# Pooled attention with two gated stages on one Trainium2 core: the attention probabilities turned by one block transpose and six DMAs through DRAM in place of twenty transposes a head pair

## Chip, cores and metric

One core of one Trainium2 chip. The metric is the device time of one execution in microseconds (us). A difference under about 0.3% (4.5 us here) is taken as no change.

## What is computed

Attention over pooled keys and values, then two dense stages; all in float32.

```
k_p = k.reshape(B, H, Sp, 8, D).mean(axis=3);  v_p likewise        # B, H, S, D = 8, 8, 576, 64; Sp = 72
attn = softmax(q @ k_p^T / sqrt(D));  out = attn @ v_p              # x: (B*S, H*D) = (4608, 512)
x = ((x @ w1) * (x @ w2) @ w3) @ w_out                              # 512 -> 1024 -> 1024 -> 512
h = x @ w_in;  y = (h * sigmoid(1.702 h)) @ w_out2                  # 512 -> 2048 -> 512
```

## The kernel before

**Stages.** Every float32 product is made of three matmuls (`mm3`, L112 to L116): each operand is split into a high part (a rounding cast by ScalarE) and a low part (the difference, by VectorE or GpSimd, L103 to L105). In a first stage weights are loaded, rounded apart (`Conv`, L127) and `w3 @ w_out` is formed (L508, L114 to L116 into `acc`). In a second, nine blocks of 512 tokens go through the gated product: for each of eight column tiles `f` 12 + 12 matmuls into `wk[0]` and `wk[1]` (L624), a copy of `wk[0]` by ScalarE (L638), the product with `wk[1]` by VectorE (L641), a split, and two tiles later 12 matmuls into `acc` (`x2_step`, L585). A third stage (L709) does the last two matrices by a Strassen-like scheme.

**The attention groups.** There are 32 groups, one for two heads of one batch entry, numbered 0 to 31. They run between the pieces of the first two stages, by `tick` (L432): a tick is called twice a column tile, and four ticks belong to a group, so that a group takes two tiles. In a group: `g0` transposes k and q in 32x32 blocks (L255, L256) and sums keys; `g1` makes ten score matmuls of 144 columns (L278), takes the maximum (L283) and subtracts it (L285); `g2` is the exponential (L294); `g3` normalizes (L300 to L303, in `s_t`, 128 tokens x 5 tiles x 160 columns) and turns the probabilities to the keys' partitions; `g4` splits the turned tiles `p0` (128 keys) and `p1` (the other 16 of 144, in 32 rows) into `ph` and `pt` (L368 to L372); `g6` multiplies by the pooled values (L380 to L383, 288 columns each) and writes x (L390, L391). `g_va` and `g_vb` (L318, L336) pool the values on GpSimd, out of one buffer `vr` that `v_load` refills.

**The turn.** Groups 0 to 3 are turned by TensorE (L351 to L361). From group 4 on, L310 to L316 issue 20 VectorE transposes a group, each of 32 partitions, 28 groups x 20 = 560.

**The order of the work.** The program is written in the order above, but a scheduler puts each engine's instructions in order by its own estimate of times. Each engine's queue then runs in order; all loads and stores of this part are issued in order by SyncE (SP), and a DMA that must wait holds those behind it. An order given below is read from the built program.

Of the kernel before, what the change touches and what calls it, by code (L numbers as in the profile page):

```python
# [7 lines left out]
F32 = mybir.dt.float32  # L8
# [4 lines left out]
ALU = mybir.AluOpType  # L13
# [4 lines left out]
P = 128  # L18
# [4 lines left out]
def pooled_attention_moe_moe2(  # L23
# [26 lines left out]
    HP = H // 2  # L50
# [18 lines left out]
    dr_p = ctx.enter_context(tc.tile_pool(name="dr", bufs=1, space=DRAM))  # L69
# [30 lines left out]
    def f32(ap):  # L100
        return ap.bitcast(F32)
# [22 lines left out]
    def sl(i, n=P):  # L124
        return slice(i * n, (i + 1) * n)
# [65 lines left out]
    with pa_ctx:  # L191
        pa = pa_ctx.enter_context(tc.tile_pool(name="pa", bufs=1))
        cv_p[0] = pa


        mask = pa.tile([P, 2, D], F32, name="mask")
        nc.gpsimd.memset(mask, 1.0 / POOL)
        nc.gpsimd.affine_select(
            out=mask[:, 0], in_=mask[:, 0], compare_op=ALU.is_gt, fill=0.0,
            base=SK, pattern=[[0, D]], channel_multiplier=-1)  # L200
        nc.gpsimd.affine_select(
            out=mask[:, 1], in_=mask[:, 1], compare_op=ALU.is_ge, fill=0.0,
            base=-SK, pattern=[[0, D]], channel_multiplier=1)
        qT = pa.tile([P, TT * P], F32, name="qT")
        nc.vector.memset(qT[:, S:], 0.0)
        kbd = pa.tile([P, 2, SK], F32, name="kbd")
# [4 lines left out]
        for t in s_ts:  # L211
# [6 lines left out]
            out=ident, in_=ident, compare_op=ALU.is_equal, fill=0.0,  # L218
            base=0, pattern=[[-1, P]], channel_multiplier=1)
# [14 lines left out]
        def g_load(n):  # L234
            if n >= NG:
                return
            b, hp = divmod(n, HP)
            g_k[n] = pa.tile([P, S], F32, name="kr", tag="raw", bufs=4).rearrange("p (g d) -> p g d", d=32)
            load_blocks(g_k[n], k, b, hp)
            g_q[n] = pa.tile([P, S], F32, name="qr", tag="raw", bufs=4).rearrange("p (g d) -> p g d", d=32)  # L240
            load_blocks(g_q[n], q, b, hp)

        def v_load(n):
            if n >= NG:
                return
            b, hp = divmod(n, HP)
            vr = v[b, 2 * hp:2 * hp + 2].rearrange("h (s u) d -> (h s) (u d)", u=POOL)
            g_v[n] = pa.tile([P, POOL * D], F32, name="vr", tag="vr")
            nc.sync.dma_start(g_v[n], vr[:P])
            nc.sync.dma_start(vtr[:KT], vr[P:])  # L250

        def g0(n):
            kr, qr = g_k.pop(n), g_q.pop(n)
            kT = pa.tile([P, S], F32, name="kT", tag="kT")
            nc.vector.transpose(out=kT, in_=kr.rearrange("p g d -> p (g d)"))  # L255
            nc.vector.transpose(out=qT[:, :S], in_=qr.rearrange("p g d -> p (g d)"))  # L256
            ks = pa.tile([P, SK], F32, name="ks", tag="ks")
# [38 lines left out]
        def g3(n):  # L296
            r, s_t = g_s.pop(n), s_of(n)
            pv = s_t[:, :, :KW].rearrange("p t (a s) -> p t a s", s=SK)
            rv = r.rearrange("p (t a) -> p t a", a=2)
            nc.vector.tensor_reduce(out=rv, in_=pv, op=ALU.add, axis=AX.X)  # L300
            nc.vector.tensor_scalar_add(r, r, 1e-9)
            nc.vector.reciprocal(out=r, in_=r)
            nc.vector.tensor_tensor(  # L303
                out=pv, in0=pv, in1=rv.unsqueeze(3).to_broadcast([P, TT, 2, SK]), op=ALU.mult)
            p0 = pa.tile([P, TT, P], F32, name="p0", tag="p0")
            p1 = pa.tile([32, TT, P], F32, name="p1", tag="p1")
            g_s[n] = (p0, p1)
            if n < NPE:
                return
            for r in range(5):  # L310
                for c in range(4):
                    nt = TT if 32 * (c + 1) <= S - (TT - 1) * P else TT - 1
                    dst = p0[32 * r:32 * r + 32] if r < 4 else p1[:32]
                    nc.vector.transpose(  # L314
                        out=dst[:, :nt, 32 * c:32 * c + 32],
                        in_=s_t[32 * c:32 * c + 32, :nt, 32 * r:32 * r + 32])  # L316

        def g_va(n):  # L318

            vr, tr = g_v.pop(n), vtr  # L320
            a = pa.tile([P, 4 * D], F32, name="va", tag="va")
            at = pa.tile([32, 4 * D], F32, name="vat", tag="vat")
            for d, s in ((a, vr), (at, tr)):
                nc.gpsimd.tensor_tensor(out=d, in0=s[:, :4 * D], in1=s[:, 4 * D:], op=ALU.add)
                nc.gpsimd.tensor_tensor(
                    out=d[:, :2 * D], in0=d[:, :2 * D], in1=d[:, 2 * D:], op=ALU.add)
                nc.gpsimd.tensor_tensor(out=d[:, :D], in0=d[:, :D], in1=d[:, D:2 * D], op=ALU.add)
            vf = pa.tile([P, 2, D], F32, name="vf", tag="vf")
            nc.gpsimd.tensor_tensor(
                out=vf, in0=a[:, :D].unsqueeze(1).to_broadcast([P, 2, D]), in1=mask, op=ALU.mult)  # L330
            vtf = pa.tile([32, D], F32, name="vtf", tag="vtf")
            nc.gpsimd.tensor_scalar_mul(vtf, at[:, :D], 1.0 / POOL)
            g_v[n] = (vf.rearrange("p a d -> p (a d)"), vtf)
            v_load(n + 1)

# [9 lines left out]
        def g4(n):  # L345
            p0, p1 = g_s.pop(n)
            if n < NPE:
                ps, s_t = banks_of(n), s_of(n)
                p0f, p1f = (t.rearrange("p t c -> p (t c)") for t in (p0, p1))
                for tt in range(4):  # L350
                    nc.tensor.transpose(ps[0][:, sl(tt)], s_t[:, tt, :P], ident)  # L351
                nc.scalar.copy(p0f[:, :T], ps[0])
                w = S - T
                nc.tensor.transpose(ps[1][:, :w], s_t[:w, 4, :P], ident[:w, :w])
                for tt in range(3):
                    nc.tensor.transpose(
                        ps[1][:32, w + tt * P:w + (tt + 1) * P], s_t[:, tt, P:], ident)
# [8 lines left out]
            s0 = p0.rearrange("p t c -> p (t c)")[:, :S]  # L366
            s1 = p1.rearrange("p t c -> p (t c)")[:, :S]
            nc.scalar.copy(ph[:, 0], s0)  # L368
            nc.gpsimd.tensor_tensor(out=ph[:, 1], in0=s0, in1=f32(ph[:, 0]), op=ALU.subtract)
            nc.scalar.copy(pt[:32], s1)  # L370
            nc.scalar.copy(pt[32:64], s1)
            nc.gpsimd.tensor_tensor(out=pt[64:96], in0=s1, in1=f32(pt[:32]), op=ALU.subtract)  # L372

        def g6(n):
            b, hp = divmod(n, HP)
# [226 lines left out]
        for blk in range(NB):  # L602
            x = [x_slot(blk, c) for c in range(KM)]
            if blk == NB - 2:

                pa_ctx.close()
                pa = pa_ctx.enter_context(tc.tile_pool(name="pc", bufs=1, reuse_waits="tile"))
# [10 lines left out]
            for f in range(NF1):  # L618
# [18 lines left out]
                a = pa.tile([P, T], F32, name="a", tag="a", bufs=2)  # L637
# [34 lines left out]
    with tc.tile_pool(name="pb", bufs=1, reuse_waits="tile") as pb, \  # L672
# [196 lines left out]
        x = x_first  # L869
# [9 lines left out]
        for k, f in enumerate(FO):  # L879
            bk = bank()  # L880
            w = ready.pop(("h", 0, f))
# [8 lines left out]
            g = moving()[:, :, 0]  # L890
# [20 lines left out]
        for pr in range(1, NPAIR + 1):  # L911
# [17 lines left out]
            for fp in range(NFP):  # L929
# [4 lines left out]
                for name, i in ORDER:  # L934
# [6 lines left out]
                    if name in PART:  # L941
                        s, h = PART[name]
                        w = ready[s, pr, 2 * fp + i][:, h]
                    else:
                        w = ready[name, pr, fp][:, i]
# [10 lines left out]
                    elif name == "M2":  # L956
# [42 lines left out]
            src = {"M5": 0, "M7": 1, "M3": 2, "M2": 3, "M4": 3, "M6": 4}  # L999
# [129 lines left out]
```

## Time and profile before

| | us |
|---|---|
| median of 3 runs (1480.33 to 1484.5) | 1483.54 |
| the profiled execution | 1480.04 |
| its span, first to last instruction | 1478.3 |
| TensorE busy in the span | 1437.1 (97%) |
| VectorE busy | 991.5 (67%) |
| ScalarE busy | 696.6 (47%) |
| GpSimd busy | 491.9 (33%) |

PE is TensorE's matmuls, PEld its weight loads, DVE VectorE, ACT ScalarE, POOL GpSimd, SPq SyncE's queue, which issues DMAs. A busy share is an average over stages that have different limits, so it has to be read stage by stage; and an engine that is always busy is at its limit only if its instructions also come at their full pace. Times in the trace count from the span's start.

### The profile page before, as it was taken

To read this page: it belongs to the slowest core of one execution; us is meant where nothing else is said; L and a number is where in the kernel's file an instruction comes from. 1 tells how busy PE (TensorE), PEld (TensorE's weight loads), DVE (VectorE), ACT (ScalarE), POOL (GpSimd) and SP (SyncE) were. 2 spreads that over 40 slices of the span, in tenths; PEclk is the share of its full clock that TensorE was granted. 3 is DMA by queue.
4 is the path that set the end of the run, shared out by engine and by line. 5 is a ranking of instruction groups with operands and counts; after the bars stand their busy time and mean duration, and the time that the engine had idled before them with its cause. 6 is when DMAs were issued, how large, how long until landed. Compare 5 with 4: busy or idle time off the path is not lost.

```text
span 1478.3 us, 19409 instructions
## 1 busy us (share of the span) xinstructions
PE 1437.1 (97%) x6536; PEld 1188.0 (80%) x6536; DVE 991.5 (67%) x1728; ACT 696.6 (47%) x1212; POOL 491.9 (33%) x589
## 2 busy tenths in 40 slices
PE   5978999999999999999999999999999999999998
PEld 3766888888888888888888887888788888888886
DVE  7889998878787877645636345783559354954554
ACT  6974444434343434366635334652455244634442
POOL 8787865555555555357743200000000000000000
PEclk9989999999999999999999999999999999999999
DMA  9992333323232321089869978877677766785665
GB/s 275 243 227 41 65 81 61 77 49 77 47 75 48 74 41 37 29 295 337 329 230 391 330 240 306 292 213 225 200 237 223 224 199 216 241 237 179 196 213 141
DMA packets 294434, 267.63 MB, mean 181 GB/s; under 512 B 201664, under 2 KB 226240, under 8 KB 294336
## 3 DMA queue, kind: packets, MB, share of 16 engines
q1 hardware_dynamic: 291648, 265.09, 60.0%
q10 hardware_dynamic: 2688, 1.31, 0.3%
q8 instruction: 52, 0.85, 0.2%
q14 instruction: 46, 0.38, 0.1%
HBM read 209.72 MB, written 56.62 MB: 180 GB/s over the span
## 4 chain that ended last, share of the span: by engine, by line
PE 82%; DVE 7%; DMA 5%; ACT 2%; POOL 2%; issue 1%; SPq 1%; DVEq 0%; ACTq 0%; POOLq 0%
PE bk L709 39%; PE wk L114 8%; PE wk L116 8%; PE wk L115 8%; PE acc L114 4%; PE acc L115 4%; PE acc L116 4%; PE wk L278 2%; DMA wud<-wt 2%; DVE s L105 1%; DVE cv L169 1%; PE bk L114 1%; PE bk L115 1%; PE bk L116 1%; POOL cv L172 1%
## 5 line engine op out<-in xcount | busy, mean ns | idle before, releaser
L709 PE MATMUL bk<-xM,st 128*128 128x512 f32 x1140 | 269.1, 390 | 1.8 <-DMA st<-wind 1.3
L709 PE MATMUL bk<-mv,st 128*128 128x512 f32 x1104 | 258.7, 389 | 0.5 <-DMA st<-wud 0.5
L709 PEld LDWEIGHTS bk<-xM,st 128*128 128x128 f32 x1140 | 213.6, 188 | 48.0 <-issue 1.9
L709 PEld LDWEIGHTS bk<-mv,st 128*128 128x128 f32 x1104 | 207.1, 188 | 44.2 <-ACT mv L104 0.9
L114 PE MATMUL wk<-s,s 128*128 128x512 f32 x576 | 227.3, 396 | 6.1 <-DVE a L641 4.1
L116 PE MATMUL wk<-s,s 128*128 128x512 f32 x576 | 225.2, 391 | 0.9 <-DVE s L105 0.9
L115 PE MATMUL wk<-s,s 128*128 128x512 f32 x576 | 225.3, 392 | 0.1
L314 DVE STREAM_TRANSPOSE p<-s_t 32x160 f32<-32x160 f32 (+1 forms) x560 | 178.3, 318 | 10.5
L115 PE MATMUL acc<-s,s 128*128 128x512 f32 x352 | 141.2, 401 | 1.0 <-POOL s L105 0.8
L116 PE MATMUL acc<-s,s 128*128 128x512 f32 x352 | 140.7, 400 | 1.6 <-DVE s L105 1.6
L114 PE MATMUL acc<-s,s 128*128 128x512 f32 x352 | 134.1, 406 | 8.1 <-DVE s L105 5.4
L114 PEld LDWEIGHTS wk<-s,s 128*128 128x128 f32 x576 | 108.5, 189 | 30.1 <-DVE a L641 5.4
L116 PEld LDWEIGHTS wk<-s,s 128*128 128x128 f32 x576 | 108.5, 188 | 23.8 <-DVE s L105 1.1
L115 PEld LDWEIGHTS wk<-s,s 128*128 128x128 f32 x576 | 108.5, 188 | 22.1 <-DVE s L391 0.5
L105 POOL TENSOR_TENSOR s<-a,s 128x512 fp32r<-128x512 f32 x56 | 73.3, 1309 | 155.2 <-ACT s L104 121.4
L105 DVE TENSOR_TENSOR mv<-g,mv 128x1024 fp32r<-128x1024 f32 x80 | 97.8, 1222 | 32.5 <-ACT mv L104 31.0
L104 ACT CAST mv<-g 128x1024 fp32r<-128x1024 f32 x80 | 84.5, 1056 | 71.3 <-PE bk L709 70.8
L172 POOL TENSOR_TENSOR cv<-cv,s 128x512 int32<-128x512 int32 x72 | 100.8, 1408 | 33.6 <-DVE cv L169 24.2
L114 PEld LDWEIGHTS acc<-s,s 128*128 128x128 f32 x352 | 67.9, 194 | 23.3 <-ACT s L104 4.7
L116 PEld LDWEIGHTS acc<-s,s 128*128 128x128 f32 x352 | 67.9, 193 | 15.8 <-DVE s L105 2.7
L115 PEld LDWEIGHTS acc<-s,s 128*128 128x128 f32 x352 | 68.0, 193 | 14.4 <-POOL s L105 2.0
L638 ACT COPY a<-wk 128x512 f32<-128x512 f32 x72 | 42.1, 585 | 68.3 <-PE wk L116 68.1
(188 smaller groups left out, 2344.6 us busy)
## 6 DMA issues: line engine op xcount, KB each, us to landing
st<-wud SPq DMA_DIRECT2D x92, 512.0 KB, 4.3
st<-wind SPq DMA_DIRECT2D x66, 512.0 KB, 4.6
st<-wind SPq DMA_DIRECT2D x84, 256.0 KB, 3.8
s<-in_moe_w_dram SPq DMA_DIRECT2D x32, 512.0 KB, 6.5
wind<-s SPq DMA_DIRECT2D x32, 512.0 KB, 5.5
s<-in_moe_w_out_dram SPq DMA_DIRECT2D x24, 512.0 KB, 6.9
s<-wud SPq DMA_DIRECT2D x20, 512.0 KB, 4.3
kr<-in_k_dram SPq DMA_DIRECT2D x128, 72.0 KB, 2.5
```

Of the source, the lines that this page charges most:

```text
L104: nc.scalar.copy(dst[:, 0], src)
L105: lo_eng.tensor_tensor(out=dst[:, 1], in0=src, in1=f32(dst[:, 0]), op=ALU.subtract)
L114: nc.tensor.matmul(o, a[:, 0, a_sl], b[:, 0, b_sl], start=first, stop=False)
L115: nc.tensor.matmul(o, a[:, 0, a_sl], b[:, 1, b_sl], start=False, stop=False)
L116: nc.tensor.matmul(o, a[:, 1, a_sl], b[:, 0, b_sl], start=False, stop=last)
L169: nc.vector.tensor_scalar(out=wu, in0=e.bitcast(U32), scalar1=3, scalar2=None, op0=ALU.logical_shift_left)
L172: nc.gpsimd.tensor_tensor(out=w.bitcast(I32), in0=w.bitcast(I32), in1=lo_w.bitcast(I32), op=ALU.add)
L278: nc.tensor.matmul(sc[half][:, i * KW:(i + 1) * KW], qT[:, sl(tt)], mov, start=True, stop=True)
L314: nc.vector.transpose(out=dst[:, :nt, 32 * c:32 * c + 32], in_=s_t[32 * c:32 * c + 32, :nt, 32 * r:32 * r + 32])
L638: nc.scalar.copy(a, pa_)
L709: nc.tensor.matmul(o, w[:, x, m], b[:, y], start=first and n == 0, stop=last and n == 2, skip_group_check=True)
```

## The change

Groups 8 to 31 (`n >= NPT`, `NPT = 2 * HP = 8`) turn their probabilities in another way; 24 of the 28 groups that were turned by VectorE. One transpose of 128 partitions (128 x 800 elements, `pT`) turns each 32x32 block in its place. Four DMAs, of 32 partitions each, write it to a DRAM tile `pD` (two buffers) in the keys' order, and two DMAs read it back as `p0` (320 KB) and `p1` (80 KB). So that tokens come out in order, q's transpose goes in two pieces into columns ordered by half and block (`turn_q`), and `g4` reads 2 x 288 of 640 columns. In these groups the two subtractions of `g4` go from GpSimd to VectorE. For all groups, `g_va` sums in place in `vr` and `vtr` (so `vr` is read until the masked product, not until the first sum), and the mask has one column, broadcast.

```diff
+        def turn_q(n, qr):
+            if n < NPT:
+                nc.vector.transpose(out=qT[:, :S], in_=qr.rearrange("p g d -> p (g d)"))
+                return
+            dst = qT.rearrange("p (t h e j) -> p e h t j", h=2, e=2, j=32)
+            src = qr.rearrange("p (h g) d -> p h g d", h=2)
+            for e, g0_, g1_ in ((0, 0, TT), (1, TT, SB // 2)):
+                nc.vector.transpose(out=dst[:, e, :, :g1_ - g0_], in_=src[:, :, g0_:g1_])
...
-            for r in range(5):
-                for c in range(4):
+            if n < NPT:
+                for r in range(5):
+                    for c in range(4):
...
+                return
+            turned = pa.tile([P, 5, TT, 32], F32, name="pT", tag="pT")
+            nc.vector.transpose(
+                out=turned.rearrange("p r t j -> p t r j"),
+                in_=s_t.rearrange("p t (r k) -> p t r k", k=32))
+            d = dr_p.tile([5, 32, 4, PC], F32, name="pD", tag="pD", bufs=2)
+            for c in range(4):
+                nc.sync.dma_start(
+                    d[:, :, c].rearrange("r k x -> k r x"),
+                    turned[32 * c:32 * c + 32].rearrange("p r t j -> p r (t j)"))
+            nc.sync.dma_start(
+                p0.rearrange("p t c -> p (t c)"), d[:4].rearrange("r k c x -> (r k) (c x)"))
+            nc.sync.dma_start(
+                p1.rearrange("p t c -> p (t c)"), d[4].rearrange("k c x -> k (c x)"))
...
-            for d, s in ((a, vr), (at, tr)):
-                nc.gpsimd.tensor_tensor(out=d, in0=s[:, :4 * D], in1=s[:, 4 * D:], op=ALU.add)
...
+            for d in (vr, tr):
+                for w in (4 * D, 2 * D, D):
+                    nc.gpsimd.tensor_tensor(
+                        out=d[:, :w], in0=d[:, :w], in1=d[:, w:2 * w], op=ALU.add)
...
-            nc.gpsimd.tensor_tensor(out=ph[:, 1], in0=s0, in1=f32(ph[:, 0]), op=ALU.subtract)
...
+            late = n >= NPT
+            lo = nc.vector if late else nc.gpsimd
...
+            nc.scalar.copy(by_half(ph[:, 0]), s0)
+            lo.tensor_tensor(out=by_half(ph[:, 1]), in0=s0, in1=by_half(f32(ph[:, 0])), op=ALU.subtract)
```

The change moves instructions on every queue. Line numbers in the orders after the change are those of the changed kernel: L332 the block transpose, L337 the writes to `pD`, L340 and L342 the reads, L399 to L402 the casts of `g4`, L400 and L403 its subtractions, L315 the normalization, L423 the x writes, L670 and L673 the copy of `wk[0]` and the product with `wk[1]` (L638 and L641 before).

**Place 1, group 19, from its normalization on.** VectorE before (12 of the 20 transposes' rows shown, with the x writes of the group ahead, L391, between them):

```order
L303 TENSOR_TENSOR s_t<-s_t,nm 128x5x144
L314 STREAM_TRANSPOSE p_3971<-s_t 32x5x32 x2
L391 TENSOR_TENSOR s_3187<-wk_72,s_3187 128x256
L314 STREAM_TRANSPOSE p_3971<-s_t 32x4x32 x2
L314 STREAM_TRANSPOSE p_3971<-s_t 32x5x32 x2
L314 STREAM_TRANSPOSE p_3971<-s_t 32x4x32 x2
L391 TENSOR_TENSOR s_3913<-wk_73,s_3913 128x288
L314 STREAM_TRANSPOSE p_3971<-s_t 32x5x32 x2
L314 STREAM_TRANSPOSE p_3971<-s_t 32x4x32 x2
```

VectorE with the change:

```order
L315 TENSOR_TENSOR s_t<-s_t,nm 128x5x144
L332 STREAM_TRANSPOSE pT<-s_t 128x5x5x32
L423 TENSOR_TENSOR s_3088<-wk_72,s_3088 128x256
L423 TENSOR_TENSOR s_3766<-wk_73,s_3766 128x288
L423 TENSOR_TENSOR s_3766<-wk_72,s_3766 128x32
L400 TENSOR_TENSOR ph<-p_3823,ph 128x576
L673 TENSOR_TENSOR a<-wk_71,a 128x512
L403 TENSOR_TENSOR pt<-p_3824,pt 32x576
L295 TENSOR_REDUCE nm<-wk_72 128x6
```

SyncE's queue in the same stretch with the change (before, it held the loads of v, k and q alone):

```order
L337 DMA pD<-pT 32x5x160 x4
L249 DMA vr<-in_v_dram 128x512
L250 DMA vtr<-in_v_dram 16x512
L340 DMA p_3823<-pD 128x640
L342 DMA p_3824<-pD 32x640
L229 DMA kr<-in_k_dram 32x18x32 x4
L229 DMA qr<-in_q_dram 32x18x32 x4
```

The transposes are gone; the subtraction L400, which waits for data that has gone through DRAM, now stands ahead of the product L673 in VectorE's queue.

**Place 2, ScalarE in group 16,** from the casts of `g4` on. Before:

```order
L368 CAST ph<-p_3419 128x576
L370 CAST pt<-p_3420 32x576
L371 CAST pt<-p_3420 32x576
L638 COPY a<-wk_70 128x512
L104 CAST s_3472<-a 128x512
```

With the change:

```order
L399 CAST ph<-p_3307 128x576
L401 CAST pt<-p_3308 32x576
L670 COPY a<-wk_70 128x512
L402 CAST pt<-p_3308 32x576
L104 CAST s_3349<-a 128x512
```

The copy of `wk[0]` stands behind casts that wait for `p0` and `p1` in both; with the change so in groups 8, 12 and 16 (behind both) and 20 and 24 (behind the first), in the other late groups ahead of them.

**Place 3, SyncE in the first stage,** from the loads of k and q for the third group on. Before:

```order
L229 DMA qr<-in_q_dram 32x18x32 x4
L249 DMA vr<-in_v_dram 128x512
L250 DMA vtr<-in_v_dram 16x512
L151 DMA s_412<-in_moe_w_dram 128x1024
L151 DMA s_447<-in_moe_w_dram 128x1024
```

With the change:

```order
L151 DMA s_648<-in_moe_w_dram 128x1024
L151 DMA s_679<-in_moe_w_dram 128x1024
L151 DMA s_755<-in_moe_w_dram 128x4x256
L249 DMA vr<-in_v_dram 128x512
L151 DMA s_786<-in_moe_w_dram 128x4x256
L250 DMA vtr<-in_v_dram 16x512
```

The second load of v comes seven weight loads later than before.

## Rows read from the trace of the kernel before

**Rows 1.** Windows: us, then busy us of each engine, PEclk, DMA share, GB/s

```profile
80.00:120.00 40.00, 32.66 (x137) 26.02 (x138) 35.85 (x51) 28.88 (x64) 35.07 (x42) 0.87 1.01 197
120.00:160.00 40.00, 35.85 (x166) 29.29 (x166) 35.62 (x73) 17.61 (x37) 33.79 (x37) 1.00 0.18 34
160.00:200.00 40.00, 39.45 (x190) 32.53 (x189) 37.25 (x94) 16.72 (x39) 26.95 (x44) 1.00 0.39 90
240.00:400.00 160.00, 160.00 (x773) 135.37 (x772) 127.38 (x315) 63.10 (x142) 86.40 (x126) 1.00 0.29 61
400.00:600.00 200.00, 200.00 (x964) 169.20 (x964) 161.54 (x395) 78.45 (x178) 101.04 (x147) 1.00 0.24 54
600.00:880.00 280.00, 279.94 (x1246) 231.77 (x1245) 140.74 (x215) 139.45 (x242) 121.46 (x94) 1.00 0.80 280
```

**Rows 2.** Timeline of DVE: normalization of group 8; last transposes of group 31

```profile
193.38 0.90 DVE L303 TENSOR_TENSOR s_t<-s_t,nm 128x720 f32<-128x720 f32 x1
...
617.65 0.96 DVE L314 STREAM_TRANSPOSE p<-s_t 32x160 f32<-32x160 f32 x3
```

**Rows 3.** Timeline of PE, group 20 and the start of 21: start, us

```profile
399.09 1.39 PE L278 MATMUL wk<-kbd,qT 128*128 128x144 f32 x10
...
417.77 1.39 PE L278 MATMUL wk<-kbd,qT 128*128 128x144 f32 x10
418.89 0.49 PE L114 MATMUL wk<-s,s 128*128 128x512 f32 x1
...
421.76 0.39 PE L114 MATMUL wk<-s,s 128*128 128x512 f32 x1
...
425.16 0.29 PE L380 MATMUL wk<-ph,vm 128*128 128x288 f32 x1
```

**Rows 4.** Groups by line and form: xcount | busy us, mean ns

```profile
L314 DVE STREAM_TRANSPOSE p<-s_t 32x160 f32<-32x160 f32 x280 | 93.5, 334 | 6.2
L314 DVE STREAM_TRANSPOSE p<-s_t 32x128 f32<-32x128 f32 x280 | 84.8, 303 | 4.3
...
L256 DVE STREAM_TRANSPOSE qT<-qr 128x576 f32<-128x576 f32 x32 | 24.6, 768 | 0.0
...
L105 DVE TENSOR_TENSOR xM<-sx,xM 128x512 fp32r<-128x512 f32 x32 | 23.0, 720 | 2.9 <-ACT xM L104 2.8
...
L105 DVE TENSOR_TENSOR s<-cv,s 128x512 fp32r<-128x512 f32 x12 | 16.0, 1336 | 1.2 <-ACT s L104 1.2
```

**Rows 5.** Timeline of DVE, same group, from its normalization

```profile
406.68 0.90 DVE L303 TENSOR_TENSOR s_t<-s_t,nm 128x720 f32<-128x720 f32 x1
...
417.65 0.69 DVE L641 TENSOR_TENSOR a<-wk,a 128x512 f32<-128x512 f32 x1 [2.13 <-ACT a L638]
```

**Rows 6.** Timeline of ACT, same group, casts and copy

```profile
416.33 0.67 ACT L371 CAST pt<-p 32x576 fp32r<-32x576 f32 x1
417.03 0.59 ACT L638 COPY a<-wk 128x512 f32<-128x512 f32 x1
```

**Rows 7.** Timeline of POOL, same group, the second subtraction

```profile
416.53 1.42 POOL L372 TENSOR_TENSOR pt<-p,pt 32x576 fp32r<-32x576 f32 x1
```

**Rows 8.** Timeline of SP's queue: four loads in group 20; x stores in group 21

```profile
401.70 1.93 SPq L229 DMA_DIRECT2D kr<-in_k_dram  x4
...
425.97 4.50 SPq L600 DMA_DIRECT2D x2d<-x2o  x3
```

**Rows 9.** DMA issues, 240 to 600 us: KB each, median us to landing

```profile
kr<-in_k_dram SPq DMA_DIRECT2D x64, 72.0 KB, 2.4
...
vr<-in_v_dram SPq DMA_DIRECT2D x18, 256.0 KB, 2.7
```

**Rows 10.** DMA issues, 640 to 930 us, where the DMA share is high

```profile
wrawd<-cv SPq DMA_DIRECT2D x16, 256.0 KB, 5.8
...
s<-x2d SPq DMA_DIRECT2D x4, 256.0 KB, 5.6
```

**Rows 11.** Timeline of POOL in the first stage, one pooling of values

```profile
92.23 0.73 POOL L324 TENSOR_TENSOR va<-vr 128x256 f32<-128x256 f32 x1 [0.28 <-DMA vr<-in_v_dram]
...
100.03 0.80 POOL L329 TENSOR_TENSOR vf<-va,mask 128x128 f32<-128x128 f32 x1
```

More of the change, by code (lines that the diff above doesn't have):

```diff
@@ L193, in pooled_attention_moe_moe2 @@
         cv_p[0] = pa
-        mask = pa.tile([P, 2, D], F32, name="mask")
+        mask = pa.tile([P, 2], F32, name="mask")
         nc.gpsimd.memset(mask, 1.0 / POOL)
         nc.gpsimd.affine_select(
-            out=mask[:, 0], in_=mask[:, 0], compare_op=ALU.is_gt, fill=0.0,
-            base=SK, pattern=[[0, D]], channel_multiplier=-1)
+            out=mask[:, 0:1], in_=mask[:, 0:1], compare_op=ALU.is_gt, fill=0.0,
+            base=SK, pattern=[[0, 1]], channel_multiplier=-1)
         nc.gpsimd.affine_select(
-            out=mask[:, 1], in_=mask[:, 1], compare_op=ALU.is_ge, fill=0.0,
-            base=-SK, pattern=[[0, D]], channel_multiplier=1)
+            out=mask[:, 1:2], in_=mask[:, 1:2], compare_op=ALU.is_ge, fill=0.0,
+            base=-SK, pattern=[[0, 1]], channel_multiplier=1)
         qT = pa.tile([P, TT * P], F32, name="qT")
@@ L250, in v_load @@
             nc.sync.dma_start(vtr[:KT], vr[P:])
+        NPT = 2 * HP
+        PC = TT * 32
+        def turn_q(n, qr):
[6 more added lines that the diff above has]
+                nc.vector.transpose(out=dst[:, e, :, :g1_ - g0_], in_=src[:, :, g0_:g1_])
         def g0(n):
@@ L255, in g0 @@
             nc.vector.transpose(out=kT, in_=kr.rearrange("p g d -> p (g d)"))
-            nc.vector.transpose(out=qT[:, :S], in_=qr.rearrange("p g d -> p (g d)"))
+            turn_q(n, qr)
             ks = pa.tile([P, SK], F32, name="ks", tag="ks")
@@ L309, in g3 @@
                 return
-            for r in range(5):
-                for c in range(4):
[L312 to L316, printed above, removed]
+            if n < NPT:
+                for r in range(5):
+                    for c in range(4):
+                        nt = TT if 32 * (c + 1) <= S - (TT - 1) * P else TT - 1
+                        dst = p0[32 * r:32 * r + 32] if r < 4 else p1[:32]
+                        nc.vector.transpose(
+                            out=dst[:, :nt, 32 * c:32 * c + 32],
+                            in_=s_t[32 * c:32 * c + 32, :nt, 32 * r:32 * r + 32])
+                return
@@ new lines, in g3 @@
+            turned = pa.tile([P, 5, TT, 32], F32, name="pT", tag="pT")
+            nc.vector.transpose(
+                out=turned.rearrange("p r t j -> p t r j"),
[5 more added lines that the diff above has]
+                    turned[32 * c:32 * c + 32].rearrange("p r t j -> p r (t j)"))
@@ L318, in g_va @@
+            nc.sync.dma_start(
+                p0.rearrange("p t c -> p (t c)"), d[:4].rearrange("r k c x -> (r k) (c x)"))
+            nc.sync.dma_start(
+                p1.rearrange("p t c -> p (t c)"), d[4].rearrange("k c x -> k (c x)"))
         def g_va(n):
             vr, tr = g_v.pop(n), vtr
-            a = pa.tile([P, 4 * D], F32, name="va", tag="va")
-            at = pa.tile([32, 4 * D], F32, name="vat", tag="vat")
-            for d, s in ((a, vr), (at, tr)):
-                nc.gpsimd.tensor_tensor(out=d, in0=s[:, :4 * D], in1=s[:, 4 * D:], op=ALU.add)
-                nc.gpsimd.tensor_tensor(
-                    out=d[:, :2 * D], in0=d[:, :2 * D], in1=d[:, 2 * D:], op=ALU.add)
-                nc.gpsimd.tensor_tensor(out=d[:, :D], in0=d[:, :D], in1=d[:, D:2 * D], op=ALU.add)
+            for d in (vr, tr):
+                for w in (4 * D, 2 * D, D):
+                    nc.gpsimd.tensor_tensor(
+                        out=d[:, :w], in0=d[:, :w], in1=d[:, w:2 * w], op=ALU.add)
@@ L328, in g_va @@
             vf = pa.tile([P, 2, D], F32, name="vf", tag="vf")
             nc.gpsimd.tensor_tensor(
-                out=vf, in0=a[:, :D].unsqueeze(1).to_broadcast([P, 2, D]), in1=mask, op=ALU.mult)
+                out=vf, in0=vr[:, :D].unsqueeze(1).to_broadcast([P, 2, D]),
+                in1=mask.unsqueeze(2).to_broadcast([P, 2, D]), op=ALU.mult)
             vtf = pa.tile([32, D], F32, name="vtf", tag="vtf")
-            nc.gpsimd.tensor_scalar_mul(vtf, at[:, :D], 1.0 / POOL)
+            nc.gpsimd.tensor_scalar_mul(vtf, tr[:, :D], 1.0 / POOL)
@@ L365, in g4, with by_half @@
             g_s[n] = (ph, pt)
-            s0 = p0.rearrange("p t c -> p (t c)")[:, :S]
-            s1 = p1.rearrange("p t c -> p (t c)")[:, :S]
-            nc.scalar.copy(ph[:, 0], s0)
-            nc.gpsimd.tensor_tensor(out=ph[:, 1], in0=s0, in1=f32(ph[:, 0]), op=ALU.subtract)
-            nc.scalar.copy(pt[:32], s1)
-            nc.scalar.copy(pt[32:64], s1)
-            nc.gpsimd.tensor_tensor(out=pt[64:96], in0=s1, in1=f32(pt[:32]), op=ALU.subtract)
+            late = n >= NPT
+            lo = nc.vector if late else nc.gpsimd
+            def by_half(ap):
+                return ap.rearrange("p (h x) -> p h x", h=2) if late else ap
+            s0, s1 = (by_half(t.rearrange("p t c -> p (t c)"))[..., :HALF if late else S]
+                      for t in (p0, p1))
+            nc.scalar.copy(by_half(ph[:, 0]), s0)
+            lo.tensor_tensor(out=by_half(ph[:, 1]), in0=s0, in1=by_half(f32(ph[:, 0])), op=ALU.subtract)
+            nc.scalar.copy(by_half(pt[:32]), s1)
+            nc.scalar.copy(by_half(pt[32:64]), s1)
+            lo.tensor_tensor(
+                out=by_half(pt[64:96]), in0=s1, in1=by_half(f32(pt[:32])), op=ALU.subtract)
         def g6(n):
```

## The prediction

> **What bounds the kernel now.** I read the windows first, to see which engine is at its limit in which stage, then the timelines of one group, to see how late each step may come.
>
> The changed groups lie late: group 8 is normalized at 193 us and the last is turned by 618.6 [rows 2], so the change's own work falls into 193 to about 630 us. From 240 to 600 us PE is busy 160.00 of 160.00 and 200.00 of 200.00 us [rows 1], at a granted clock of 1.00, the level of 2.4 GHz. A busy PE need not be at full pace, since matmul ends are modelled, so I check the pace in the timeline [rows 3]: from the first matmul into `wk[1]` at 421.76 to the first L380 at 425.16 come 15 matmuls of 512 columns, 3.40 / 15 = 0.227 us each, 2.26 columns a ns, close to the clock. Score matmuls start a group at 399.09 and the next at 417.77: a period of 18.68 us, in which 72 such matmuls take 72 x 0.227 = 16.3 and the 10 + 8 small ones the other 2.4. PE waits for nothing here. VectorE is busy 161.54 of 200 us and GpSimd 101.04; they are not the limit. A faster VectorE has nothing to give to this stretch; what has to be asked is whether the new path makes PE wait.
>
> Before 200 us PE does lose time: 40 - 32.66 = 7.3, 40 - 35.85 = 4.2 and 40 - 39.45 = 0.6 us in three windows [rows 1], together 12.0 us. But groups 0 to 7 turn as before there.
>
> **The change part by part.** I use the clock of group 20 [rows 3 to 8]; its normalization ends at 406.68 + 0.90 = 407.58.
>
> *Removed from VectorE:* 20 transposes a group, 10 of 334 ns and 10 of 303 ns [rows 4], 6.4 us. *Added:* the block transpose. From 160 columns in 334 ns to 576 in 768 ns a column costs 434 / 416 = 1.04 ns [rows 4], so 800 columns take 768 + 224 x 1.04 = 1.00 us. q's transpose in two pieces of 320 and 256 columns: 0.50 + 0.43 instead of 0.77, so +0.16. Two subtractions of 576 columns that GpSimd did: the row of 512 columns with both inputs in SBUF says 0.72, the one of the first stage, where GpSimd is busy for 34 to 35 of 40 us, 1.34 [rows 1, 4]; times 576/512 that is 0.81 to 1.50. I take 0.81, because GpSimd has lost just these two pieces and is mostly idle at that time. Sum per group: -6.4 + 1.0 + 0.16 + 1.6 = -3.6 us, -87 us of VectorE for 24 groups; GpSimd loses 2 x 1.42 [rows 7] x 24 = -68 us. All of it lies beside a PE that is busy throughout: 0 us of the time.
>
> On this price the Trainium skill ("SBUF — State Buffer", section "SBUF: two separate sides") says that a VectorE instruction with two SBUF inputs and a GpSimd instruction take turns on a shared port pair, the loser blocked for the whole instruction; by it the two subtractions would cost up to one GpSimd instruction more each (the 1.34 us row agrees in size), and the sum would still be 0, since 1.3 us more fits before 421.76.
>
> *The new path to `ph` and `pt`.* Normalization ends at 407.58 + 0.16 = 407.74, the turn at 408.75. SP issues four DMAs in 1.93 us, 0.48 each [rows 8]; the last of the four writes starts at about 408.8 + 3 x 0.48 = 410.25. A write to `pD` is 100 KB. This program has no such write in this stretch; the nearest rows are the 72 KB loads into 32 partitions, 2.4 us from issue to landing, and the 256 KB loads, 2.7 [rows 9]. I take 2.4: all is in DRAM at 412.65. The reads must wait for that; `p0` (320 KB) by the same two rows takes 2.8, `p1` 2.4: both are there at about 415.6. The bounds are 2.4 + 2.7 below and 2.7 + 3.0 above, so 415.5 to 416.1; far off stand 5.8 + 5.6, what a write to DRAM and a reading back take at a DMA share of 0.80 [rows 1, 10], which would make it 421.8. The share in this stretch is 0.24 to 0.29 [rows 1], and the extra 0.8 MB a group in 18.68 us is 44 GB/s on top of 54, so the near rows are the ones to use. Then come three casts of 0.67 by ScalarE [rows 6] (416.3, 417.0, 417.6) and the subtractions by VectorE (417.1, 417.9). Before, GpSimd ended at 416.53 + 1.42 = 417.95 [rows 7]. The two paths come out even: 6.6 us of transposes became 1.0 of transposing and 6.8 of DMA, and two serial subtractions of 1.4 became two of 0.8.
>
> *Who waits for that.* PE needs the pieces at 425.16 [rows 3], 7.2 us later. Closer are the instructions queued behind them. ScalarE's copy of `wk[0]` (0.59 us, [rows 6]) must be done before PE writes `wk[0]` again at 418.89; where it stands behind the first two casts (groups 8, 12, 16) it ends at 417.6, 1.3 us to spare; behind one cast (20, 24) 2.0. VectorE's product with `wk[1]` (0.69, [rows 5]) must be done by 421.76; behind both subtractions it ends at 418.6, 3.2 to spare; behind one (eleven groups) more. In the six groups in which a block ends, stores of x hold part of the writes in SP's queue: they were issued up to 4.50 us after 425.97 [rows 8], 12.7 us into the group; 1 us for the last pair, 2.4 + 2.8 and 2.3 for casts and subtractions give 21.2 us, against 26.1 for L380 (425.16 - 399.09), and there copy and product stand ahead. So 0 us again.
>
> *Queues passed.* SP issues six more DMAs a group, 144 in all; a group's 16 now take 16 x 0.48 = 7.7 of 18.68 us, and k and q come two groups ahead. *Values:* the same eight GpSimd instructions a group; 0 us of work. *Mask:* smaller, in the first microseconds, behind the first weight load; 0.
>
> **Sum:** 0. The profiled execution took 1480.0, 3.5 under the median of the runs; I carry the 0 over to the median: 1483.5 us.
>
> **The rivals.** "No change" means within 0.3%, 4.5 us: 1479.0 to 1488.0.
>
> *A. Another order of the first stage gains.* The scheduler orders the whole program anew, and PE's order differs from about the third group on, in the stretch where 12.0 us are lost [rows 1]. Half of that back is 1477.5, all of it 1471.5. For: the loss is there, with VectorE at 35 to 38 of 40 us. Against: from 80 to 120 us the DMA share is 1.01 [rows 1], and nothing loads less; the work there is the same. 0.22.
>
> *B. Values hold up the first stage: slower.* `vr` is now read until the masked product, so the load of the next values must wait for that, and SP holds weight loads behind it. In one pooling of the first stage the first sum ended at 92.96 and the masked product at 100.83 [rows 11], 7.9 us later. If SP stands for that long once, and the weights loaded ahead run out, PE waits: 1483.5 + 7.9 = 1491.4. It decides from the point where the conversion has used up what was loaded. For: the DMA share of 1.01, so that lost issue time is not made up. Against: the order puts the second load of v seven weight loads later, so that SP may reach it after the product. A new order that merely loses as much as A might gain belongs here too. 0.18.
>
> *C. The turned data come late.* If the four writes ran one after another, the last would land 4 x 2.4 = 9.6 after the first issue and not 3.9: 5.7 late. The copies would then miss 418.89 by 4.4 us (three groups) and 3.7 (two), the products 421.76 by about 1.7 (eleven): 13 + 7 + 19 = 39 us; a stall gives the next group more room, so half to all, 20 to 39, about 1513. It decides from 1.3 us of lateness. Against: four loads of k into 32 partitions are issued 0.48 apart, and their median to landing is 2.4 [rows 8, 9], so they overlap. The Trainium skill ("DMA: Bandwidth & Descriptors", section "Rules for kernel authors") speaks for it: transfers to separate partition ranges serialize, one over 128 partitions is to be used, and under 64 KB one pays mostly overhead; by this rule the writes would be the dear part. The rows of k do not show four of them taking turns. 0.10.
>
> That the change does not do what it says is excluded: the order holds 24 block transposes, and the old ones for groups 4 to 7 alone.
>
> **How the numbers follow.** My forecast, nothing on the path, has 0.50, A 0.22, B 0.18, C 0.10. So faster by over 0.3% 0.22, within 0.50, slower 0.28. The range leaves out the far half of A (under 1474) and most of C (over 1497): 1474 to 1497. The unknown DMA times within their near bounds do not widen it.
>
> **What would show it.** Right: from 240 to 600 us PE busy throughout with groups 18.7 us apart, VectorE down to about 60% of that stretch, GpSimd to about a third; `p0` landing some 7 us after the block transpose, and PE's wait for `wk` empty. Wrong: PE idle before L114 into `wk` in groups 8, 12 and 16 (C), a longer stretch before 200 us with SP standing before a load of `vr` (B), or less idle time there (A).

## The result and the profile after

The changed kernel takes 1499.28 us (1498.1 to 1499.44) against 1484.02 (1480.33 to 1484.84) of the kernel before beside it: ratio 1.0109, 95% interval 1.0095 to 1.0124, about 15 us slower. Forecast was no change, 1483.5, range 1474 to 1497.

The stretch on which the sum rests came out as forecast. Windows of the changed kernel, columns as in [rows 1]:

```profile
80.00:120.00 40.00, 26.22 (x104) 20.00 (x104) 28.64 (x42) 27.49 (x57) 34.48 (x35) 0.81 0.77 163
120.00:160.00 40.00, 30.80 (x125) 24.17 (x126) 31.51 (x77) 15.99 (x37) 31.99 (x46) 0.77 0.27 52
160.00:200.00 40.00, 40.00 (x195) 33.92 (x194) 35.46 (x82) 18.02 (x42) 25.81 (x38) 1.00 0.31 59
240.00:400.00 160.00, 160.00 (x773) 135.60 (x772) 94.24 (x174) 61.86 (x140) 62.68 (x103) 1.00 0.45 104
400.00:600.00 200.00, 200.00 (x965) 169.44 (x964) 117.33 (x217) 76.75 (x176) 75.65 (x129) 1.00 0.43 104
600.00:880.00 280.00, 280.00 (x1255) 232.66 (x1254) 138.43 (x204) 139.66 (x248) 121.72 (x99) 1.00 0.76 274
```

From 240 to 600 us TensorE is busy throughout, as before, while VectorE does 44 us less work from 400 to 600 and GpSimd 25 less. The loss is ahead of that: 26.22 and 30.80 us of work where [rows 1] has 32.66 and 35.85, and with a lower granted clock.

Where the time is lost can be read from the same event in both traces. The second block's first store of `x2d` goes out at 290.7 us in place of 276.5, 14.2 later; the third stage's first matmul at 782.4 in place of 769.1, 13.3 later; the end is 19.3 later. So there are two losses: some 14 us before 200 us, and some 6 in the third stage, where the diff changes no line. The two sizes are of one profile each: the profiled execution of the kernel before took 1480.04 us, 4.0 under its median, that of the changed kernel 1499.33, so the profiles are 19.3 us apart and the medians 15.3.

**One late group.** Timeline of the changed kernel, group 19, to compare with [rows 5 to 8]: start, us, engine, what it was waiting for.

```profile
402.84 0.90 DVE L315 TENSOR_TENSOR s_t<-s_t,nm 128x720 f32<-128x720 f32 x1
403.77 1.01 DVE L332 STREAM_TRANSPOSE pT<-s_t 128x800 f32<-128x800 f32 x1
...
404.81 1.78 SPq L337 DMA_DIRECT2D pD<-pT  x4
...
408.23 0.34 SPq L340 DMA_DIRECT2D p<-pD  x1
...
411.89 0.67 ACT L399 CAST ph<-p 128x576 fp32r<-128x576 f32 x1 [3.38 <-DMA p<-pD]
...
412.60 0.90 DVE L400 TENSOR_TENSOR ph<-p,ph 128x576 fp32r<-128x576 f32 x1 [7.04 <-ACT ph L399]
413.42 0.68 DVE L673 TENSOR_TENSOR a<-wk,a 128x512 f32<-128x512 f32 x1
414.13 0.75 DVE L403 TENSOR_TENSOR pt<-p,pt 32x576 fp32r<-32x576 f32 x1
```

```profile
pD<-pT SPq DMA_DIRECT2D x76, 100.0 KB, 1.9
p<-pD SPq DMA_DIRECT2D x20, 320.0 KB, 3.3
...
p<-pD SPq DMA_DIRECT2D x20, 80.0 KB, 3.1
```

The second fence is the list of DMA issues from 240 to 600 us, in the columns of [rows 9]. The turn takes 1.01 us, the writes land in 1.9, the first read goes out 3.4 us after the turn's end and `p0` is cast 7.1 us after it. Four writes, 0.45 apart, are all in by then, since that read waits for them; one after another they would have taken 4 x 1.9 = 7.6. The Trainium skill ("DMA: Bandwidth & Descriptors", section "Rules for kernel authors") says that two transfers to disjoint partition halves serialize. Here the four did not take turns with their whole time to landing; whether their bytes do, no run here shows.

**The first stage.** Timeline of the changed kernel from the load of group 3's values to its products with them and on, over all engines:

```profile
99.72 0.44 SPq L249 DMA_DIRECT2D vr<-in_v_dram  x1
...
102.96 1.19 POOL L350 TENSOR_TENSOR vr<-vr 128x256 f32<-128x256 f32 x1
...
113.66 0.76 DVE L257 STREAM_TRANSPOSE qT<-qr 128x576 f32<-128x576 f32 x1
...
114.57 2.74 PE L290 MATMUL wk<-kbd,qT 128*128 128x144 f32 x10 [4.45 <-DVE qT L257]
...
120.16 0.58 POOL L353 TENSOR_TENSOR vf<-vr,mask 128x128 f32<-128x128 f32 x1
...
120.80 0.28 ACT L363 CAST vm<-vf 128x128 fp32r<-128x128 f32 x1
...
121.13 0.61 PE L412 MATMUL acc<-ph,vm 128*128 128x288 f32 x1 [3.83 <-ACT vm L363]
...
124.69 0.85 PE L414 MATMUL acc<-ph,vm 128*128 128x288 f32 x2 [2.23 <-POOL vm L364]
...
125.44 6.65 DVE L327 STREAM_TRANSPOSE p<-s_t 32x160 f32<-32x160 f32 x20
...
132.12 0.76 DVE L423 TENSOR_TENSOR s<-acc,s 128x288 fp32r<-128x288 f32 x2
...
132.93 0.79 PE L115 MATMUL wk<-s,s 128*128 128x512 f32 x1 [4.73 <-DVE s L423]
```

The load is issued at 99.72, the sums run from 102.96 to 120.7 between other work on GpSimd, TensorE waits for the values at 121.13 and 124.69, and the x of the first block, and with it the gated product, comes late (132.93). In the kernel before, the same sums ran from 92.23 to 100.83 [rows 11].

Not all of the waiting is for the values. From 60 to 200 us TensorE is idle for 25.2 of 140 us, 13.9 in the kernel before. Of the 25.2, 6.1 go to the values of group 3. 4.45 go to the transpose of q (L257), which stands in VectorE's queue behind a shift of 4.14 us (L169, shown in the last section), and 4.73 to the x write (L423), which stands there behind another group's twenty transposes, 6.65 us together. Which of these waits would go if the values came early is not shown by this trace alone.

While TensorE waited its clock fell: the ten scores take 2.74 us where [rows 3] has 1.39. In the window from 112 to 136 us it is busy for 9.54 us at a granted clock of 0.50, the level of 1.2 GHz; at 1.00 that work takes half as long, so up to 4.8 us of the 14 are the clock's, an estimate from this window.

### The profile page after: what moved, and what is told of

Read it like the earlier page. It is cut to its first block, busy times and chain, and to the rows that moved or that the text cites. A ratio compares the mean times of both kernels' runs of the same rounds, so it can differ in the third digit from the quotient of the medians.

```text
span 1497.6 us, 19232 instructions
## 1 busy us (share of the span) xinstructions
PE 1441.6 (96%) x6536; PEld 1192.0 (80%) x6536; DVE 892.8 (60%) x1344; ACT 694.4 (46%) x1212; POOL 427.1 (29%) x541
## 4 chain that ended last, share of the span: by engine, by line
PE 85%; DMA 6%; DVE 4%; ACT 2%; issue 1%; SPq 1%; POOL 1%; DVEq 0%; ACTq 0%; POOLq 0%
PE bk L741 39%; PE wk L114 9%; PE wk L116 9%; PE wk L115 9%; PE acc L116 4%; PE acc L114 4%; PE acc L115 4%; PE wk L290 2%; DMA wud<-wt 1%; DMA s<-in_moe_w_dram 1%; PE bk L116 1%; PE bk L114 1%; PE bk L115 1%; DMA st<-wind 1%; DVE s L105 1%
## 5 line engine op out<-in xcount | busy, mean ns | idle before, releaser
L114 PEld LDWEIGHTS wk<-s,s 128*128 128x128 f32 x576 | 108.7, 189 | 24.5 <-ACT a L670 1.2
L172 POOL TENSOR_TENSOR cv<-cv,s 128x512 int32<-128x512 int32 x72 | 97.7, 1364 | 36.9 <-DVE cv L169 21.4
L400 DVE TENSOR_TENSOR ph<-p,ph 128x576 fp32r<-128x576 f32 x24 | 24.3, 1011 | 129.3 <-ACT ph L399 129.3
L670 ACT COPY a<-wk 128x512 f32<-128x512 f32 x72 | 42.2, 586 | 113.9 <-PE wk L116 112.3
```

The source lines that it names most:

```text
L114: nc.tensor.matmul(o, a[:, 0, a_sl], b[:, 0, b_sl], start=first, stop=False)
L172: nc.gpsimd.tensor_tensor(out=w.bitcast(I32), in0=w.bitcast(I32), in1=lo_w.bitcast(I32), op=ALU.add)
L400: lo.tensor_tensor(out=by_half(ph[:, 1]), in0=s0, in1=by_half(f32(ph[:, 0])), op=ALU.subtract)
L670: nc.scalar.copy(a, pa_)
```

## The experiments

The theory: `g_va` sums in place, so the one buffer `vr` is released later, the next values come later, and the first stage loses. Its rivals: any new order of the first stage loses as much; or the turn through DRAM does it.

**e1, the mask alone.**

```diff
-        mask = pa.tile([P, 2, D], F32, name="mask")
+        mask = pa.tile([P, 2], F32, name="mask")
...
```

> The kernel before with the one-column mask alone. TensorE's order is that of before up to its 360th instruction, then moves a little. Values theory (the in-place sums make the first stage's loss): same as before, ratio 0.997 to 1.003, TensorE busy 32 to 34 us from 80 to 120 us and 35 to 37 from 120 to 160. Order theory (any new order of the first stage costs some 15 us): 1490 to 1500 us, ratio above 1.005.

Ratio 1.0006 (0.9993 to 1.0019), TensorE busy 31.46 and 34.54 us, just under the 32 and 35 expected: this other order costs little.

**e2, the values alone** (in-place sums and the mask; turn as before).

```diff
-            for d, s in ((a, vr), (at, tr)):
+            for d in (vr, tr):
+                for w in (4 * D, 2 * D, D):
+                    nc.gpsimd.tensor_tensor(
+                        out=d[:, :w], in0=d[:, :w], in1=d[:, w:2 * w], op=ALU.add)
...
```

> The kernel before with the in-place sums and the one-column mask, turn as before. TensorE's order is that of the changed kernel up to its 558th instruction, so for the whole first stage. Values theory: the first stage loses as in the changed kernel, TensorE busy about 26 us from 80 to 120 us and 31 from 120 to 160, time 1493 to 1500 us, ratio 1.007 to 1.011. Turn theory (the DRAM path or its subtractions make the loss): 1484 us, ratio 0.997 to 1.003, busy 33 and 36 us.

Ratio 1.0083 (1.0071 to 1.0095), and the first stage of the changed kernel, window for window (columns as in [rows 1]):

```profile
80.00:120.00 40.00, 26.17 (x104) 20.31 (x104) 30.13 (x44) 28.28 (x59) 35.28 (x36) 0.84 0.78 164
120.00:160.00 40.00, 31.06 (x118) 24.09 (x119) 30.09 (x72) 15.90 (x36) 31.78 (x45) 0.73 0.23 45
```

**e3, the late turn alone** (values in a buffer of their own).

```diff
-            for d in (vr, tr):
+            a = pa.tile([P, 4 * D], F32, name="va", tag="va")
+            at = pa.tile([32, 4 * D], F32, name="vat", tag="vat")
+            for d, s in ((a, vr), (at, tr)):
...
```

> The changed kernel with the values summed as before (a buffer of its own, so the raw values are free after the first sum; room found by placing the tail of the values in unused partitions of the tile of p1). TensorE's order is that of the mask-only kernel up to its 547th instruction. Values theory: about the time of before, 1480 to 1488 us; up to 1490 if the extra 4 us that the changed kernel lost after 880 us come from the DRAM path. Turn theory: 1493 to 1500 us.

Ratio 1.0025 (1.0014 to 1.0036). The two parts add up: 0.83% + 0.25% = 1.08%, the change costs 1.09%. In e3 the third stage begins 1.0 us earlier than in the kernel before and the end is 3.5 later: its whole loss lies in the third stage.

**e4, in-place sums with two buffers.**

```diff
-            g_v[n] = pa.tile([P, POOL * D], F32, name="vr", tag="vr")
+            g_v[n] = pa.tile([P, POOL * D], F32, name="vr", tag="vr", bufs=2)
...
-            nc.sync.dma_start(vtr[:KT], vr[P:])
+            nc.sync.dma_start(vtrs[n % 2][:KT], vr[P:])
...
```

> The changed kernel with in-place sums kept, and two buffers for the raw values in place of one, so that the load of the next values does not wait for the masked product. If the wait of that load makes the loss: 1480 to 1488 us, TensorE busy 32 or more from 80 to 120 us. If the loss comes from the order that the scheduler chose and not from the wait: another order again, anything from 1480 to 1500 us, and a result near 1497 would speak against the wait.

Ratio 1.0024 (1.0011 to 1.0038): the loss of the first stage is gone, with another order again.

```profile
80.00:120.00 40.00, 32.92 (x136) 25.34 (x137) 30.53 (x52) 29.86 (x69) 37.73 (x45) 0.87 0.94 207
120.00:160.00 40.00, 35.03 (x156) 28.55 (x156) 35.96 (x73) 17.41 (x35) 33.64 (x36) 0.96 0.20 37
```

**e8, the loads of values on ScalarE's queue,** one buffer.

```diff
-            nc.sync.dma_start(g_v[n], vr[:P])
+            nc.scalar.dma_start(g_v[n], vr[:P])
...
```

> The changed kernel with one value buffer and in-place sums kept, but the loads of the values issued by ScalarE's queue, so that they don't stand behind the loads of k and q in SP's queue. If the place in SP's queue makes the values late: the products with the values of group 3 begin near 103 us (121 in the changed kernel) and the time is 1485 to 1489 us, of which 3.5 belong to the pD tiles. If the one buffer itself does (the load cannot start before the masked product, whoever issues it): 1493 to 1500 us. ScalarE standing at such a load would be a loss of its own, to be seen as its idle time.

Ratio 1.0107 (1.0092 to 1.0122), the products of group 3 at 119.2 us. The time lies in the range expected for the one buffer, but the run tells nothing apart: group 0's products already begin at 76.6 us (57.8 in the changed kernel), because the whole order changed and TensorE does 30.86 of 40 us from 40 to 80 where the changed kernel does 36.99.

**e12, early sums, late release.** One element a partition of `vr` is read once more after the masked product.

```diff
...
+            nc.gpsimd.tensor_tensor(out=last[:, :1], in0=vr[:, :1], in1=vf[:, 0, :1], op=ALU.add)
+            nc.gpsimd.tensor_tensor(out=last[:32, 1:], in0=tr[:, :1], in1=vtf[:, :1], op=ALU.add)
```

> The mask-only kernel, values summed in a buffer of their own, with two additions of one column more a group, each of which reads the raw values (or their tail) together with the finished masked product, so that the raw buffer is released as late as by in-place sums. Release theory: the load of the values of group 3 goes out near 100 us, the products with them begin near 120 and the time is 1493 to 1500 us. Other theory (the in-place sums themselves, or the particular order that they led to): 1484 to 1489 us, the two small additions costing GpSimd under 1 us a group.

Ratio 1.0145 (1.012 to 1.017), 1503.75 us, 3.8 above the range expected. Its timeline, and under it that of e1, which lacks these additions:

```profile
102.78 0.45 SPq L249 DMA_DIRECT2D vr<-in_v_dram  x1
...
117.33 0.39 POOL L329 TENSOR_TENSOR vf<-va,mask 128x128 f32<-128x128 f32 x1
...
123.60 0.61 PE L383 MATMUL acc<-ph,vm 128*128 128x288 f32 x1
```

```profile
89.49 0.44 SPq L249 DMA_DIRECT2D vr<-in_v_dram  x1
...
101.57 0.75 POOL L329 TENSOR_TENSOR vf<-va,mask 128x128 f32<-128x128 f32 x1
...
104.64 0.40 PE L380 MATMUL acc<-ph,vm 128*128 128x288 f32 x1 [2.43 <-ACT vm L338]
```

The late release alone moves the load by 13 us and the products by 19; not all of the 19 is the values, since TensorE stands 3.23 us for q at 122.19, just before these products, and not for `vm`; for `vt` it waits 3.23 us later on, at 129.60. With e4 it shows that the late release is the cause, not the in-place sum. A control that reads `va` in place of `vr`, with the same two small additions (GpSimd busy 496.4 us, in e1 490.3), was not run.

How a late release becomes a loss is shown only in part. The load of group 3's values does not stand at a semaphore in SP's queue: in the changed kernel it follows 0.1 us behind the load of q ahead of it. The order, made with the later release in it, has it further down the queue, behind sets of four loads of k and q of which one takes 3.60 us ([rows 8] has 1.93), and its sums further down GpSimd's. A later load does stand: SP waits 13.6 us for `vtf` of group 4 before it issues the load of group 5's values at 139.33. No loss shows behind it: from 136 to 200 us TensorE is busy for 64.00 of 64.00 us.

**The third stage.** The premise, which no trace shows since none holds addresses: each of the 24 `pD` tiles gets DRAM of its own, 24 x 409,600 = 9,830,400 bytes, and that moves the tiles of the later stages. e5 moves them by as much in the kernel before, e10 by 8 MiB.

```diff
-    x2_d = [dr_p.tile([P, KM, T], F32, name=f"x2d{b}", tag=f"x2d{b}") for b in range(NB)]
+    x2_d = [dr_p.tile([1328 if b == 0 else P, KM, T], F32, name=f"x2d{b}", tag=f"x2d{b}")[:P] for b in range(NB)]
```

(e10 has 1152 for 1328.)

> The kernel before, every instruction in its order, with 9,830,400 bytes left free behind the first x2d tile in DRAM, so that the DRAM tiles of the second and third stage lie as far up as the 24 pD tiles push them in the changed kernel. Address theory (the 3.4 us lost after 960 us come from where the tiles lie): 1486 to 1488 us, ratio 1.002 to 1.003, median landing of the wud reads 4.5 us in place of 4.2. Rival (they come from the late turn in another way): ratio 0.999 to 1.001, 4.2 us.

> The kernel before, every instruction in its order, with the DRAM tiles behind the first x2d tile moved up by 8,388,608 bytes (four times 2 MiB) in place of 9,830,400. If any move costs: ratio 1.002 to 1.004. If it is how the tiles lie against a power of two: ratio 0.999 to 1.001, median landing of the wud reads 4.2 us.

e5: ratio 1.0034 (1.0021 to 1.0047), 1488.88 us, 0.9 above the range expected of the address theory. e10: 0.9988 (0.9975 to 1.0000). The instructions and their order on every engine are the same in all three. DMA issues from 960 to 1460 us (KB each, median us to landing) of the kernel before, of e5 and of e10:

```profile
st<-wud SPq DMA_DIRECT2D x81, 512.0 KB, 4.2
...
st<-wind SPq DMA_DIRECT2D x62, 256.0 KB, 3.6
```

```profile
st<-wud SPq DMA_DIRECT2D x81, 512.0 KB, 4.7
...
st<-wind SPq DMA_DIRECT2D x62, 256.0 KB, 4.0
```

```profile
st<-wud SPq DMA_DIRECT2D x80, 512.0 KB, 4.2
...
st<-wind SPq DMA_DIRECT2D x62, 256.0 KB, 3.5
```

So the reads of `wud` and the smaller ones of `wind` land 0.4 to 0.5 us later when their tiles lie 9,830,400 bytes further up, and not when they lie 8 MiB further up; the 512 KB reads of `wind` take 4.4, 4.2 and 4.2 and don't tell. In the changed kernel the two figures are 4.5 and 3.9. From the third stage's first matmul to the end, e5 takes 3.2 us longer than the kernel before, e10 0.3, e1 1.3, e2 0.8, e3 4.5, e4 4.4, e8 5.2 and the changed kernel 6.0. These lengths, of one profile each, do not tell by themselves: e12, whose tiles are not moved, takes 2.9 longer too. The 256 KB reads of `wind` do tell: their median is 3.9 to 4.2 us in the five kernels with `pD` tiles or the move of e5 (the changed kernel, e3, e4, e5, e8), and 3.5 to 3.8 in the other nine.

**e6, no `pD` at all:** e4 (two value buffers) with the turned data sent through `wud` tiles, which are not in use yet.

```diff
-            d = dr_p.tile([5, 32, 4, PC], F32, name="pD", tag="pD", bufs=2)
+            d = wu_d[6 + n % 2].rearrange("p f a m -> (p f a m)")[:20 * 32 * PC].rearrange(
+                "(r k c x) -> r k c x", k=32, c=4, x=PC)
```

> The kernel with two value buffers, but the turned data go through wud tiles that are not in use before the third stage, so that there is no pD tile. TensorE's order is that of the run with two value buffers. Address theory: the loss after 960 us shrinks from 6.7 to 3 us, time about 1484 us, ratio 0.999 to 1.001. Rival: as the run with two value buffers, ratio 1.002 to 1.003.

Ratio 0.9996 (0.9983 to 1.0009), against 1.0024 for e4, from which it differs by `pD` alone: with both losses removed the new turn neither gains nor costs, which is the forecast for it.

**e9, how close the late path is.** e6 with a second copy in DRAM between the writes and the reads.

```diff
...
+            nc.sync.dma_start(
+                d2.rearrange("r k c x -> (r k) (c x)"), d.rearrange("r k c x -> (r k) (c x)"))
+            d = d2
```

> The kernel with two value buffers and no pD tile, its late groups sent through DRAM twice (a copy from one wud tile to another between the writes and the reads), so that the turned data come some 3 to 5 us later. In the changed kernel the last subtraction ends 9.7 us after the block transpose and the products with the values begin at 16.5, so 6.8 us are to spare there; the prediction's slack at the copy of wk[0] was 1.3 to 2.0 us where the copy stands behind the casts. If the slack of the products decides: no change, 1482 to 1486 us. If the copies and products in the queues behind decide (rival C with 3 to 5 us of lateness): five to eleven groups lose 1 to 3 us each, 1490 to 1510 us.

Ratio 1.0257 (1.0244 to 1.0271), 38 us; 1521.38, above both ranges expected. `ph` is cast some 10.3 us after the turn, 3.3 later. Windows (columns as in [rows 1]), TensorE's waits from 230 to 640 us (total, times, longest), and the timeline of one of them:

```profile
240.00:400.00 160.00, 149.57 (x706) 123.37 (x707) 85.42 (x157) 56.54 (x130) 59.50 (x97) 1.00 0.48 118
```

```profile
PE wk L420 <- DVE s_t L299: 20.8, 15, 2.8
PE wk L420 <- ACT ph L407: 1.9, 2, 1.8
```

```profile
422.23 0.76 DVE L408 TENSOR_TENSOR ph<-p,ph 128x576 fp32r<-128x576 f32 x1 [7.89 <-ACT ph L407]
...
425.45 0.57 DVE L299 TENSOR_TENSOR s_t<-wk,nm 128x432 f32<-128x432 f32 x1
...
426.16 0.37 PE L420 MATMUL wk<-ph,vm 128*128 128x288 f32 x1 [1.39 <-DVE s_t L299]
```

TensorE's products with the values go into the bank that the next group's scores must leave first. L299 takes them out, and stands in VectorE's queue behind L408, which waits for the data from DRAM, and the instructions behind that. With 3.3 us of lateness a group loses 38 / 24 = 1.6, so the slack is about 1.7 us, a rough estimate from these two numbers: TensorE's waits in that stretch add up to 24.5 us, and the rest of the 38 is not accounted for.

**e7 and e11, candidates:** the turn from group 4 on, through `wud` tiles, with two value buffers (e7) or sums in a buffer of their own (e11).

```diff
...
-        NPT = 2 * HP
+        NPT = HP
...
```

> The same kernel with the new turn from group 4 on in place of group 8. In the first stage VectorE loses another 4 x 3.6 = 14 us of work from 120 to 200 us, where TensorE lost 7.3 us with two value buffers. If VectorE sets the pace there: 1477 to 1482 us. If the order of the queues does, or the data through DRAM come late while weights are converted: 1483 to 1490 us.

> The candidate to beat both: values summed in a buffer of their own as before, the new turn from group 4 on, the data through wud tiles. It keeps the gain of VectorE and leaves out both losses found. If VectorE's 20 transposes hold back the first stage: 1476 to 1481 us; if not, 1481 to 1486.

Ratios 0.9992 (0.9979 to 1.0006) and 1.0009 (1.0000 to 1.0019); 1482.04 us is the edge between the two ranges expected of e7, 1484.07 lies in the second of e11. In e7 VectorE's relief does reach TensorE from 120 to 160 us (40.00 of 40 busy, [rows 1] has 35.85), but TensorE loses 2.2 us from 200 to 240 (37.82 of 40), and the third stage begins only 0.7 us earlier. No version here beats the kernel before by more than 0.3%.

## Why the prediction was wrong

- **What bounds it: right.** TensorE stays busy from 240 to 600 us, and 98.7 us less work of VectorE (87 forecast) gain nothing; e6 shows it by itself.
- **The prices of the late path: right in sum, in part by luck.** The turn 1.01 us (1.00 forecast), the two pieces of q 0.49 and 0.43 (0.50 and 0.43), writes 1.9 (2.4), reads 3.3 and 3.1 (2.8 and 2.4); the cast starts 7.1 us after the turn (6.85). The writes lie under their bounds of 2.4 to 2.7 and the larger read over its 2.7 to 3.0; the two misses cancel. The subtractions take 0.99 and 0.75 us on average (0.81 each), inside the bounds of 0.81 and 1.50.
- **The slack: near in size by chance, wrong in place.** 1.3 us was forecast at ScalarE's copy; e9 finds about 1.7 at the score bank, through VectorE's queue. That wait was not on the list of who waits behind the late subtraction. So rival C did not occur, but is close.
- **The step that failed: "Values: the same eight GpSimd instructions a group; 0 us of work".** The work is the same; what moves is when `vr` is free, and that price was left out of the sum and given to rival B. The order on record already had the second load of v seven weight loads later, and this was counted against B, as a reason that SP would not stand, and not as values that come later. e2 measures it at 0.83%, 12.3 us, of which B had 7.9. B also had another way: weights that run out behind a standing SP. The last three weight loads of that stretch were in fact issued from 100.7 us on, before from 102.5, and SP's standing of 13.6 us before a load of `vr`, which B named as its sign, comes after them, and no wait of TensorE over 0.5 us follows it. Late were the values, the products of group 3 and the first block of the gated product, with waits for q and for VectorE's queue among them; and the clock, which fell while TensorE waited, is part of it. How the 12.3 us divide among these is open.
- **A term that was missing: where DRAM tiles lie.** The sum asked what the new DMAs cost beside others, and not what a new DRAM tile does to the old ones. e3 measures 0.25%, e5 0.34%, 3.7 to 5 us. With the values' 12.3 us alone the time would be 1495.8, inside the range; both losses take it past 1497.
- B's other clause, "a new order that merely loses", is half of it: the loss comes through the order, but not through any order. The eight other kernels whose raw values are free early (e9 aside), in several orders, are between 0.9988 and 1.0034; the four with one buffer released late are at 1.0083 to 1.0145.

Open: how the place of a DRAM tile acts on its reads. In e7 and e11, which have no `pD`, the third stages take 3.2 and 4.7 us longer than before, and in e12 2.9; no trace shows where their tiles lie, and what lengthens them was not tried.

## What to carry to other kernels

When an edit reuses a buffer in place, ask when that buffer is released and what its next load stands behind, even if the instructions stay the same; price that in the stage with no slack, not in the one the change is made for. A new DRAM tile may move others: compare the landing times of old transfers, and test the edit with the tiles moved and nothing else. Work taken off an engine that is not the limit was worth nothing here (e6), and a longer path that hides is to be tested by making it longer still, to learn how far it is from deciding.

## What the hardware showed that was not expected

Most reads of weights in the third stage, the same in size and order, landed 0.4 to 0.5 us later (median) after a move by 9,830,400 bytes, not after one by 8,388,608 (e5, e10).

An elementwise VectorE instruction of 128x512 that usually takes under a microsecond took 4.14 us at one place of the changed kernel (3.73 at the same place of e2; the longest in the kernel before is 3.77), and TensorE's wait for q stands behind it. The first line is the view of tile `cv` (min, median, max in ns), the others the timeline:

```profile
L169 DVE TENSOR_SCALAR cv<-cv x40: 357/492/4140, 5.0 to 134.3; 128x512 uint32<-128x512 uint32 x40
```

```profile
109.23 4.14 DVE L169 TENSOR_SCALAR cv<-cv 128x512 uint32<-128x512 uint32 x1
...
109.35 1.27 POOL L172 TENSOR_TENSOR cv<-cv,s 128x512 int32<-128x512 int32 x1
110.59 1.25 POOL L105 TENSOR_TENSOR s<-cv,s 128x512 fp32r<-128x512 f32 x1
111.81 1.27 POOL L172 TENSOR_TENSOR cv<-cv,s 128x512 int32<-128x512 int32 x1
```

It ends at 113.37, just after the three GpSimd instructions beside it (113.08), which ran without a gap. The Trainium skill ("SBUF — State Buffer", section "Who interferes with whom") has the loser of the port pair that both engines share blocked for one whole instruction; here it looks like three, though no run here isolated it.
